# Six steps of 768 tokens instead of nine of 512 in the last phase of a fused attention and mixer kernel, with layer two after layer one and partly by seven block products

## The chip, the cores and the metric

The kernel runs on one core of a Trainium2 chip. The metric is the device time of one execution in microseconds (us); the median of three runs is shown beside a profile of one execution. The engines are TensorE (PE; PEld is its weight load, which runs beside the matmuls), VectorE (DVE), ScalarE (ACT), GpSimd (POOL) and SyncE (SP). In this kernel POOL and SP mostly issue transfers (DMAs).

## The reference

Three stages follow each other on 8 sequences of 576 tokens and 512 channels, all in float32:

```
p_packed = softmax(p k^T / 8) v          # 32 packed keys per head, 8 heads of 64
x        = softmax(q p_packed^T / 8) p_packed
xk, xr   = mu * x + (1 - mu) * x_prev    # x_prev: the token before
x        = sigmoid(xr @ w_r) * (relu(xk @ w_k)^2 @ w_v)         # 512 -> 1024 -> 512
u        = x + (x^T @ U @ V)^T           # mixing over tokens, rank 32
out      = u + relu(u @ w_ch1) @ w_ch2   # 512 -> 2048 -> 512
```

## The kernel before

The work stands in one program whose order is set by a planner (class `Plan`). The program adds operations with the tiles that they read and write; `emit` then plays a list schedule over its own estimates of durations and transfer times, and each engine gets its instructions in the order in which that schedule took them. An engine keeps to its order at run time, so an instruction that is not ready holds all that stand behind it. A tile pool with n buffers gives out its oldest buffer again when the readers of the old tile are done.

Every float32 operand of a large product is split into a high and a low part of type fp32r (`split`: a copy, mostly on ACT, and a subtraction on DVE), and each product runs three passes, high by high, high by low, low by high (`PASS`).

*Phase 1* (0 to about 697 us) is attention and the first mixer, in 12 chunks of 384 token columns. Its last chunks also prepare the last phase: the float64 weights are cast, and `make_ws` forms seven combinations of 128 x 256 blocks of `w_ch1` per pair f of hidden blocks, splits them and stores them in DRAM (`ws_d`).

*Phase 2* (from about 697 us) is the last two lines of the reference, over 36 tiles of 128 tokens in `NQ` = 9 steps q of four tiles. `load_u`, `h_block` and `t_block` (lines 1280 to 1329) bring x, add the token mixing (tile names psh, u) and turn u so that channels lie on partitions (ux, uq_d, ut; in the first step by matmuls, pst); `operands` (L1331) forms seven combinations of half-size blocks and splits them (ob). Then, for each f of 8 (loop at L1526):

- Layer one is a 2 x 2 block product with seven products in place of eight. `product` (L1355) does one as 6 matmuls (2 halves of the contraction by 3 passes) of 256 columns: 128 hidden units by 256 tokens, the weights (tile wb) from `ws_d`, 256 KB for each product, issued by POOL into a ring of 11 buffers (`load_ws`, L1246). Sums and copies of the seven results (tile tmp) give the four blocks of the hidden layer.
- `hidden` (L1370) applies relu and splits each block (tile hid).
- Layer two is plain: `c2_block` (L1378) multiplies a block of hid by the 128 x 512 rows of `w_ch2`, which are split once and stay in SBUF (w2). These are 3 passes of 512 columns per token tile and hidden block, accumulated over the 16 hidden blocks in four PSUM banks that hold a whole step.

So one f is 42 matmuls of 256 columns and 24 of 512, and both kinds stand side by side in PE's order: layer two of one f is done with layer one of the next. In the profile psc names the PSUM tiles of both layers.

## Time and profile before

| | |
|---|---|
| three runs | 1465.65, 1471.7 and 1472.11 us, median 1471.7 |
| profiled execution | span 1469.3 us from the first to the last instruction; no time around the span is given |
| PE busy | 1435.3 us, 98% of the span, 9104 matmuls |
| PEld, DVE, ACT busy | 85%, 67% and 49% of the span |
| psc matmuls | 1728 of 512 columns (layer two) and 3024 of 256 columns (layer one) |
| DMA | 294.53 MB; 132.15 MB of them by POOL's queue |

How to read it. The mean of one matmul is its length from start to end, and neighbours overlap; what one costs in a stream is the distance from start to start. Busy time of a group is the union of its matmuls' spans. A wait is named by what ended it. The share of DMA is summed over queues, so it can pass 1 when two queues have packets under way on the same engine.

### The profile page before, as it was taken

How to read it: one execution, taken by the hardware profiler on the slowest of the kernel's cores; microseconds unless marked ns; L12 is line 12 of the kernel's file. 1: busy time of each engine (PE TensorE's matmuls, PEld its weight loads, DVE VectorE, ACT ScalarE, POOL GpSimd, SP SyncE). 2: the span in 40 equal slices, each digit the busy share in tenths (PEclk: the TensorE clock that was granted, in tenths of full speed). 3: DMA queues.
4: the chain of work that ended last, by engine and by line, in shares of the span. 5: the costliest groups of instructions: out<-in, count | busy, mean ns of one | idle time of the engine just before them, and what ended most of it. 6: DMA issues, size and time to landing. Idle time of an engine off the chain costs nothing.

```text
span 1469.3 us, 25583 instructions
## 1 busy us (share of the span) xinstructions
PE 1435.3 (98%) x9104; PEld 1254.8 (85%) x9104; DVE 987.4 (67%) x2142; ACT 713.9 (49%) x1522; POOL 269.4 (18%) x519
## 2 busy tenths in 40 slices
PE   6789999999999999999999999999999999999998
PEld 5557988788888888888999999999999999999997
DVE  6877977788798888895665565556546554554633
ACT  5668656666676677764443333323333332323322
POOL 0000000000000000010333333333333343333331
PEclk9989999999999999999999999999999999999999
DMA  8963344655654477791999898899988889879763
GB/s 230 244 182 145 109 106 119 201 162 150 181 154 149 149 236 266 249 279 46 315 267 241 224 232 219 214 256 232 229 225 216 206 214 252 209 215 236 202 177 81
DMA packets 235725, 294.53 MB, mean 200 GB/s; under 512 B 91216, under 2 KB 126352, under 8 KB 235600
## 3 DMA queue, kind: packets, MB, share of 16 engines
q1 hardware_dynamic: 163024, 160.76, 37.9%
q0 software_dynamic: 72576, 132.15, 35.8%
q8 instruction: 73, 1.20, 0.4%
q14 instruction: 52, 0.43, 0.1%
HBM read 231.94 MB, written 60.89 MB: 199 GB/s over the span
## 4 chain that ended last, share of the span: by engine, by line
PE 90%; DVE 3%; DMA 3%; ACT 1%; SPq 1%; issue 1%; DVEq 0%; ACTq 0%
PE psc L197 51%; PE psv L197 12%; PE psk L197 12%; PE psr L197 6%; PE psat L197 4%; PE psat L209 2%; SPq L319 1%; DMA st<-in_moe_w_k_dram 1%; PE psu L197 1%; DMA w_d<-m 1%; PE psh L197 1%; DMA kin<-in_k_dram 0%; ACT a L233 0%; DMA st<-in_moe_w_ch_dram 0%; DVE a L264 0%
## 5 line engine op out<-in xcount | busy, mean ns | idle before, releaser
L197 PE MATMUL psc<-w,hid 128*128 128x512 f32 x1728 | 420.1, 391 | 0.0
L197 PEld LDWEIGHTS psc<-ob,wb 128*128 128x128 f32 x3024 | 387.1, 191 | 13.3
L197 PE MATMUL psc<-ob,wb 128*128 128x256 f32 x3024 | 391.6, 283 | 0.0
L319 POOL DMA_DIRECT2D wb<-ws_d x504 | 267.4, 531 | 647.0 <-PE psc L197 375.4
L197 PEld LDWEIGHTS psc<-w,hid 128*128 128x128 f32 x1728 | 314.8, 188 | 59.7 <-DVE hid L273 0.3
L233 ACT ACTIVATE hid<-tmp 128x256 fp32r<-128x256 f32 x216 | 131.3, 675 | 231.1 <-DVE tmp L254 231.1
L197 PE MATMUL psk<-xk,wk 128*128 128x384 f32 x1056 | 205.2, 339 | 0.1
L197 PE MATMUL psv<-wv,kk 128*128 128x512 f32 x783 | 201.5, 394 | 0.0
L197 PEld LDWEIGHTS psk<-xk,wk 128*128 128x128 f32 x1056 | 185.4, 188 | 9.7 <-issue 1.9
L197 PEld LDWEIGHTS psv<-wv,kk 128*128 128x128 f32 x783 | 144.4, 188 | 28.9 <-issue 0.8
L273 DVE SCALAR_TENSOR_TENSOR hid<-tmp,hid 128x256 fp32r<-128x256 f32 x216 | 126.7, 633 | 54.8 <-ACT hid L233 54.1
L273 DVE SCALAR_TENSOR_TENSOR hid<-psc,hid 128x256 fp32r<-128x256 f32 x72 | 45.3, 629 | 170.3 <-ACT hid L233 170.3
L254 DVE TENSOR_TENSOR tmp<-tmp,psc 128x256 f32<-128x256 f32 x288 | 112.9, 409 | 60.2 <-PE psc L197 59.8
L233 ACT ACTIVATE hid<-psc 128x256 fp32r<-128x256 f32 x72 | 45.8, 636 | 158.5 <-PE psc L197 158.5
L197 PE MATMUL psr<-wr,xr 128*128 128x512 f32 x414 | 110.7, 403 | 0.2
L197 PEld LDWEIGHTS psr<-wr,xr 128*128 128x128 f32 x414 | 76.5, 191 | 18.5 <-issue 1.7
L288 ACT ACTIVATE tmp<-psc 128x256 f32<-128x256 f32 x144 | 57.2, 397 | 59.4 <-PE psc L197 51.5
L233 ACT ACTIVATE sq<-psk 128x384 f32<-128x384 f32 x96 | 46.4, 489 | 68.1 <-PE psk L197 67.5
L311 POOL MEMSET x<- 128x8 f32 x4 | 0.5, 113 | 384.8 <-DVE m L270 384.5
L254 DVE TENSOR_TENSOR kk<-sq,kk 128x384 fp32r<-128x384 f32 x87 | 47.5, 550 | 26.7 <-ACT kk L288 26.4
L270 DVE SCALAR_TENSOR_TENSOR m<-x,mu_t,m 128x384 f32<-128x384 f32 x88 | 52.0, 607 | 2.3 <-ACT m L233 2.2
L233 ACT ACTIVATE m<-x,om_t 128x384 f32<-128x384 f32 x88 | 50.6, 606 | 4.0 <-DVE xr L254 2.9
(176 smaller groups left out, 1590.4 us busy)
## 6 DMA issues: line engine op xcount, KB each, us to landing
wb<-ws_d POOLq DMA_DIRECT2D x504, 256.0 KB, 4.0
st<-in_moe_w_ch_dram SPq DMA_DIRECT2D x32, 512.0 KB, 5.1
ws_d<-wb SPq DMA_DIRECT2D x56, 256.0 KB, 3.6
x_d<-xo SPq DMA_DIRECT2D x16, 576.0 KB, 3.7
x_d<-x SPq DMA_DIRECT2D x36, 256.0 KB, 2.6
kin<-in_k_dram SPq DMA_DIRECT2D x32, 256.0 KB, 4.9
vin<-in_v_dram SPq DMA_DIRECT2D x32, 256.0 KB, 5.5
w_d<-m SPq DMA_DIRECT2D x32, 256.0 KB, 4.0
```

The source lines that it names most:

```text
L197: self.nc.tensor.matmul(o, l, r, start=start, stop=stop, **k)
L209: self.nc.tensor.transpose(out.get(), in_.get(), ident.get())
L233: self.nc.scalar.activation(o, in_.get(), func, **k)
L254: return self.elem(engs, lambda e, o, x, y: e.tensor_tensor(out=o, in0=x, in1=y, op=op), out, [a, b], self.TT, cls)
L270: ("dve",), lambda e, o, x, y, z: e.scalar_tensor_tensor(out=o, in0=x, scalar=z, in1=y, op0=op0, op1=op1), out, [a, b, s], {"dve": (1.042, ...
L273: ("dve",), lambda e, o, x, y: e.scalar_tensor_tensor(out=o, in0=x, scalar=s, in1=y, op0=op0, op1=op1), out, [a, b], self.TT, cls)
L288: self.nc.scalar.activation(o, i, AF.Copy)
L311: (self.nc.gpsimd if eng == "pool" else self.nc.vector).memset(o, 0.0)
L319: (self.nc.sync if eng == "sp" else self.nc.gpsimd).dma_start(out=o, in_=i)
```

## The change

Phase 2 goes in `NS` = 6 steps s of six tiles (768 tokens); a token half is three tiles, 384 columns.

- `window_a` does layer one of a whole step first: the same seven products per f, 6 matmuls of 384 columns each. The hidden blocks stay in SBUF as float32 (tile hid; blocks 11, 12, 21, 22 are token half by hidden block of the pair, for four groups g of two f). The moving operand is now read as three tiles of 32-element pieces (t, a, r).
- Layer two follows. In steps 0 and 1 `window_b_plain` does it as before, 512 columns a pass, with `w2` loaded and split again in each of these steps, and beside it `make_t` forms seven combinations per pair of `w_ch2` blocks and stores them in DRAM (`t_d`).
- In steps 2 to 5 `window_b` does it by seven block products in seven stages (PSUM tiles psX, psY, psZ, psW). A stage is four units g; a unit splits one 128 x 768 hidden combination (`halves_split`, tile sp, 3 buffers) and runs 18 matmuls of 256 columns. The weights come from `t_d`. Sums over hidden blocks (hid) run ahead of the stages, and `into` adds results to u in SBUF after a stage.
- Weights of both layers come in transfers of 512 KB (two products or one unit) into a ring of 6 buffers (`load_w`).
- The operands of the next step (`operand_steps`) are formed at the end of `window_a` and through layer two. Phase 1 keeps its matmuls; tiles of weights share pools in groups (wA, wB, wC), mixed inputs are allotted in pairs, and six u tiles in place of four are prepared before phase 2.

In PE's order, one f of phase 2 stood like this before (a stretch past the middle; hid and wb name the operands of layer two and layer one):

```order
L197 MATMUL psc_11704<-ob,wb 128x256 x6
L197 MATMUL psc_11713<-ob,wb 128x256 x6
L197 MATMUL psc_11753<-ob,wb 128x256 x6
L197 MATMUL psc_11131<-w_10_8099,hid 128x512 x3
L197 MATMUL psc_11145<-w_10_8099,hid 128x512 x3
```

At the passage from layer one to layer two of a late step it now stands like this (ring is a weight transfer, sp a split hidden combination):

```order
L197 MATMUL psc_13571<-ob,ring 128x384 x6
L197 MATMUL psX<-ring,sp 128x256 x5
L197 MATMUL psc_13570<-ob,ring 128x384 x6
L197 MATMUL psX<-ring,sp 128x256 x67
L197 MATMUL psY<-ring,sp 128x256 x58
L197 MATMUL psX<-ring,sp 128x256 x2
L197 MATMUL psY<-ring,sp 128x256 x14
L197 MATMUL psX<-ring,sp 128x256 x38
L197 MATMUL psZ<-ring,sp 128x256 x2
L197 MATMUL psX<-ring,sp 128x256 x18
L197 MATMUL psZ<-ring,sp 128x256 x2
L197 MATMUL psX<-ring,sp 128x256 x14
```

The two layers no longer alternate. Where two or so matmuls of a later stage stand in the middle of psX, the planner saw psX not ready there.

On DVE, one f of phase 2 stood like this before (tmp are sums of layer one, hid the low parts of the split, u and ux the preparation of the next step):

```order
L254 TENSOR_TENSOR tmp<-tmp,psc_14997 128x256
L273 SCALAR_TENSOR_TENSOR hid<-psc_14988,hid 128x128x2
L254 TENSOR_TENSOR tmp<-tmp,psc_14997 128x256
L254 TENSOR_TENSOR tmp<-tmp,psc_15030 128x256
L254 TENSOR_TENSOR tmp<-tmp 128x256
L273 SCALAR_TENSOR_TENSOR hid<-tmp,hid 128x128x2 x2
L254 TENSOR_TENSOR tmp<-tmp,psc_14997 128x256
L254 TENSOR_TENSOR u<-psh,u 128x512
```

In the second and third stage of a late step DVE now has this (sp is the low part of a split, hid a sum over hidden blocks, u a result added):

```order
L254 TENSOR_TENSOR sp<-hid,sp 128x768 x2
L254 TENSOR_TENSOR u<-u,psX 128x2x256 x2
L273 SCALAR_TENSOR_TENSOR hid<-hid 128x768
L254 TENSOR_TENSOR u<-u,psX 128x256 x2
L254 TENSOR_TENSOR sp<-hid,sp 128x768
L273 SCALAR_TENSOR_TENSOR hid<-hid 128x768
L254 TENSOR_TENSOR u<-u,psX 128x2x256
L254 TENSOR_TENSOR sp<-hid,sp 128x768
L254 TENSOR_TENSOR hid<-hid 128x768
L254 TENSOR_TENSOR u<-u,psX 128x256
L273 SCALAR_TENSOR_TENSOR sp<-hid,sp 128x768
L273 SCALAR_TENSOR_TENSOR hid<-hid 128x768
```

Between two splits that PE waits for stand sums that are needed later only. The core of the diff:

```diff
-    NQ = NBP * NI // 4
-    vx_p, st_p, wb_p, tr_p = rpools = [Pool(bufs=n) for n in (1, 6, 11, 3)]
+    NS = NBP * NI // 6
+    ring_p, vx_p, st_p, turn_p = rpools = [Pool(bufs=n) for n in (6, 1, 4, 1)]
...
+    def put_split(homes, src, dst):
+        if not piece:
+            piece.extend(pieces(*next(homes)))
+        t, hi, lo = piece.pop(0)
+        split(hi, lo, src)
+        plan.dma(dst, t.rearrange("p a c -> p (a c)").bitcast(F32))
+
...
+    def make_t(f, homes):
+        homes = iter(homes)
+        b11, b12, b21, b22 = [t[:, h * 256:(h + 1) * 256] for t in raw_pair(w2_d, f) for h in range(2)]
+        t1, t2, t3, t4 = [temp("sums")[:, 0:256] for _ in range(4)]
+        plan.tt(t1, b12, b11, sub)
+        plan.tt(t2, b22, t1, sub)
+        plan.tt(t3, b12, b22, sub)
+        plan.tt(t4, b21, t2, sub)
+        g, h = divmod(f, 2)
+        for i, src in enumerate((b11, b21, b22, t4, t1, t2, t3)):
+            put_split(homes, src, t_d[i][g].at(h)[:, h * 512:(h + 1) * 512])
-    def load_ws(f, i):
-        t = plan.tile(wb_p, [P, 2, 256], F32R, "wb", parts=(0, 1))
-        plan.dma(t.rearrange("p a c -> p (a c)"), ws_d[f].at(i)[:, i * 512:(i + 1) * 512], eng="pool")
-        return t
+    def load_w(src):
+        t = plan.tile(ring_p, [P, 2, 2, 256], F32R, "ring")
+        plan.dma(t.rearrange("p n a c -> p (n a c)"), src, eng="pool")
+        return t
...
-        ops[q] = [o11] + [whole(x) for x in (t2, t1, b21, b12, b22, b11)]
+        for i, src in enumerate((b11, t2, t1, b21, b12, b22, b11)):
+            yield
...
+            if i == 6:
+                plan.tt(b11, b21, t2, sub)
+            hi, lo = [half(t, n).rearrange("p (a c) -> p a c", a=4) for n in range(2)]
+            plan.cls = 2 if s and i > 2 else 1
+            plan.copy(hi, src, ("act",) if s else ("act", "dve"))
+            plan.tt(lo, src, hi, sub)
+            plan.cls = 1
+            ops[s].append(t)
...
-        n = 0
-        for k in range(2):
-            for wi, a in PASS:
-                plan.mm(ps, half(w, wi)[:, k * P:(k + 1) * P],
-                        half(x, a).rearrange("p (a k c) -> p k a c", a=4, k=2)[:, k],
+    def product(s, f, i, ps, fresh):
+        n, e = divmod(ws_at[f, i], 2)
+        if e == 0:
+            wpair[0] = load_w(ws_d[n])
+        w, x = wpair[0][:, e], ops[s][i]
+        out = ps[:, 0:CW]
+        c = 0
+        for k in range(2):
+            for wi, a in PASS:
+                plan.mm(out, w[:, wi, k * P:(k + 1) * P],
+                        half(x, a).rearrange("p (a k t r) -> p k t a r", a=4, k=2, t=3)[:, k],
+                        start=(fresh and c == 0), stop=(c == 5), skip_group_check=True)
+                c += 1
+        return out
...
-    def hidden(src):
-        t = plan.tile(mix_p, [P, 2, CW], F32R, "mx", parts=(0, 1), name="hid")
-        hi, lo = [half(t, i)[:, 0:256].rearrange("p (t c) -> p c t", t=2) for i in range(2)]
-        src = src.rearrange("p (c t) -> p c t", t=2)
-        plan.act(hi, src, AF.Relu)
-        plan.stt(lo, src, 0.0, hi, ALU.max, sub)
-        return t
+    def window_a(s, prep):
+        hb = {}
...
+        for f in range(NF):
+            g, e = divmod(f, 2)
+            h11, h12, h21, h22 = [hb[b, g][e] for b in ("11", "12", "21", "22")]
+            ba = new_bank("psc1")
+            a = product(s, f, 0, ba, True)
+            p1, p5 = temp("p1"), temp("p5")
+            plan.copy(p1, a, ("act",))
+            if last:
+                tail(*last)
+            bb = new_bank("psc1")
+            b = product(s, f, 1, bb, True)
+            plan.tt(h21, p1, b, add)
+            bc = new_bank("psc1")
+            c = product(s, f, 2, bc, True)
+            plan.copy(p5, c, ("act",))
+            product(s, f, 3, ba, False)
+            plan.act(h11, a, AF.Relu)
+            product(s, f, 4, bb, False)
+            plan.tt(h22, p1, b, add)
+            plan.tt(h22, h22, p5, add)
+            product(s, f, 5, bc, False)
+            plan.tt(h21, h21, c, add)
+            if s >= NPLAINB:
+                plan.stt(h21, h21, 0.0, h11, ALU.max, sub)
+            last = (f, bb, p1)
+            for fn in prep.get(f, ()):
+                fn()
+        tail(*last)
+
+    def halves_split(src, relu):
+        t = plan.tile(sp_p, [P, 2, 768], F32R, "sp", parts=(0, 1))
+        hi, lo = [half(t, n).rearrange("p (f c) -> p f c", f=2) for n in range(2)]
+        if relu:
+            plan.act(hi, src, AF.Relu)
+            plan.stt(lo, src, 0.0, hi, ALU.max, sub)
+        else:
+            plan.copy(hi, src, ("act",))
+            plan.tt(lo, src, hi, sub)
+        return [half(t, n) for n in range(2)]
...
-        for t in range(2):
-            for i, (a, wi) in enumerate(PASS):
-                plan.mm(acc[q, th][t], half(h, a)[:, t * P:(t + 1) * P], half(w, wi),
-                        start=(fresh and i == 0), stop=(last and i == 2))
+        def into(u, col, name, op=add):
+            cs = slice(col * 256, (col + 1) * 256)
+            x = accs[name]
+            u01, u2 = u[0][:, :, cs], u[1][:, cs]
+            plan.tt(u01, u01, x[0].rearrange("p (t c) -> p t c", t=2), op)
+            plan.tt(u2, u2, x[1][:, 0:256], op)
...
+        stages = (("X", 0, "11", True), ("Y", 6, "21", True), ("X", 1, "12", False), ("Z", 4, "11", True),
+                  ("Y", 3, "22", False), ("Z", 5, "21", False), ("W", 2, "12", True))
+        for n, (name, ti, blk, fresh) in enumerate(stages):
+            if fresh:
+                accs[name] = [new_bank("ps" + name) for _ in range(2)]
+            acc = accs[name]
+            for g in range(NF // 2):
+                h11, h12, h21, h22 = [hb[b, g][2] for b in ("11", "12", "21", "22")]
+                if n == 3:
+                    plan.tt(h11, h21, h11, add)
+                elif n == 6:
+                    plan.stt(h12, h12, 0.0, h21, ALU.max, sub)
+                x = halves_split(hb[blk, g][2], n in (2, 4))
+                if n == 2:
+                    plan.stt(h21, h22, 0.0, h21, ALU.max, add)
+                w = load_w(t_d[ti][g])
+                for e in range(2):
+                    for t in range(3):
+                        o = acc[t // 2][:, t % 2 * 256:(t % 2 + 1) * 256]
+                        for c, (a, wi) in enumerate(PASS):
+                            plan.mm(o, x[a][:, e * CW + t * P:e * CW + (t + 1) * P], w[:, e, wi],
+                                    start=(fresh and g == 0 and e == 0 and c == 0 and t != 1),
+                                    stop=(g == NF // 2 - 1 and e == 1 and c == 2), skip_group_check=True)
+            if n == 0:
+                into(u0, 1, "X")
+                into(u1, 0, "X")
+                into(u1, 1, "X")
+            elif n == 1:
+                into(u1, 1, "Y")
+            elif n == 2:
+                into(u0, 0, "X")
+            elif n == 3:
+                into(u1, 0, "Z", sub)
...
+            next_op()
...
+                    x = halves_split(hb[("11", "12", "21", "22")[2 * th + k], g][2], (th, k) != (0, 0))
+                    for e in range(2):
+                        for t in range(3):
+                            for c, (a, wi) in enumerate(PASS):
+                                plan.mm(acc[3 * th + t], x[a][:, e * CW + t * P:e * CW + (t + 1) * P], half(w[e], wi),
+                                        start=(g == 0 and k == 0 and e == 0 and c == 0),
+                                        stop=(g == NF // 2 - 1 and k == 1 and e == 1 and c == 2))
+                next(more, None)
+                if k == 0 and NPLAINB < NS:
+                    make_t(s * NF // NPLAINB + g, [(3, sp_p, "sp")] + [(2, ust_p, "ust")] * 2)
...
-    for q in range(NQ):
-        for f in range(NF):
+    for s in range(NS):
+        prep = {f: [] for f in range(NF)}
+        more = iter(())
+        if s + 1 < NS:
+            T0 = 6 * s + 6
+            for T in range(T0, T0 + 6):
+                load_u(T)
+            for n in range(6):
+                T = T0 + n
+                if T % NI == 0:
+                    prep[n].append(lambda T=T: load_xu(T // NI))
+                prep[n + 1].append(lambda T=T: h_block(T))
+                prep[n + 2].append(lambda T=T: t_block(T))
+        window_a(s, prep)
+        if s + 1 < NS:
+            more = operand_steps(s + 1)
+            next(more)
+        (window_b if s >= NPLAINB else window_b_plain)(s, more)
+        for _ in more:
+            pass
```

## Rows read from the trace of the kernel before

**Rows 1.** From the page: busy time of each engine, share of the span, instructions.

```profile
PE 1435.3 (98%) x9104; PEld 1254.8 (85%) x9104; DVE 987.4 (67%) x2142; ACT 713.9 (49%) x1522; POOL 269.4 (18%) x519
```

**Rows 2.** The chain that ended last: start us, us, what, number of matmuls.

```profile
177.76 4.18 PE psk L197 x24
...
725.07 10.52 PE psc L197 x66
...
746.58 52.59 PE psc L197 x330
```

**Rows 3.** PE's groups by form: matmuls, columns, count, busy us, mean ns, idle us.

```profile
L197 PE MATMUL psc<-w,hid 128*128 128x512 f32 x1728 | 420.1, 391 | 0.0
L197 PE MATMUL psc<-ob,wb 128*128 128x256 f32 x3024 | 391.6, 283 | 0.0
L197 PE MATMUL psk<-xk,wk 128*128 128x384 f32 x1056 | 205.2, 339 | 0.1
```

**Rows 4.** PE in time order, fourth step: start us, us, what, count.

```profile
1001.88 0.40 PE L197 MATMUL psh<-X,vst 128*128 128x512 f32 x1
1002.11 2.32 PE L197 MATMUL psc<-ob,wb 128*128 128x256 f32 x18
1004.27 2.91 PE L197 MATMUL psc<-w,hid 128*128 128x512 f32 x12
1007.02 2.31 PE L197 MATMUL psc<-ob,wb 128*128 128x256 f32 x18
1009.17 2.91 PE L197 MATMUL psc<-w,hid 128*128 128x512 f32 x12
```

**Rows 5.** POOL's waits: us in total, times, longest.

```profile
POOL wb L319 <- PE psc L197: 375.4, 145, 45.2
```

**Rows 6.** Stretches: busy us of each engine (instructions), clock, DMA share, GB/s.

```profile
697.00:734.00 37.00, 37.00 (x234) 33.41 (x233) 24.28 (x51) 16.26 (x33) 13.75 (x26) 1.00 1.13 310
734.00:770.00 36.00, 36.00 (x230) 32.77 (x229) 22.77 (x48) 14.54 (x30) 12.70 (x24) 1.00 1.13 264
868.00:953.00 85.00, 85.00 (x533) 77.00 (x532) 45.79 (x97) 27.86 (x54) 29.61 (x56) 1.00 0.87 222
```

**Rows 7.** DMA queues from 703 to 715 us: packets, bytes, mean rate.

```profile
DMA packets 2338, 4.22 MB, mean 352 GB/s; under 512 B 285, under 2 KB 285, under 8 KB 2337
```

**Rows 8.** DMA issues: count, size of each, median us to landing.

```profile
wb<-ws_d POOLq DMA_DIRECT2D x504, 256.0 KB, 4.0
...
uq_d<-ux SPq DMA_DIRECT2D x16, 512.0 KB, 5.1
...
xa<-xu_d SPq DMA_DIRECT2D x32, 64.0 KB, 5.8
```

**Rows 9.** DVE's groups by form: shape, count, busy us, mean ns, idle us.

```profile
L254 DVE TENSOR_TENSOR tmp<-tmp,psc 128x256 f32<-128x256 f32 x288 | 112.9, 409 | 60.2 <-PE psc L197 59.8
...
L254 DVE TENSOR_TENSOR kk<-sq,kk 128x384 fp32r<-128x384 f32 x87 | 47.5, 550 | 26.7 <-ACT kk L288 26.4
...
L254 DVE TENSOR_TENSOR u<-psh,u 128x512 f32<-128x512 f32 x36 | 24.6, 683 | 0.6 <-PE psh L197 0.4
L254 DVE TENSOR_TENSOR u<-psc,u 128x512 f32<-128x512 f32 x36 | 24.5, 688 | 17.7 <-PE psc L197 17.6
...
L215 DVE STREAM_TRANSPOSE ux<-u 128x512 f32<-128x512 f32 x32 | 22.3, 696 | 0.1
...
L254 DVE TENSOR_TENSOR ob<-sums,ob 128x512 fp32r<-128x512 f32 x18 | 12.3, 687 | 0.0
...
L254 DVE TENSOR_TENSOR a<-a,s 128x640 f32<-128x640 f32 x8 | 6.5, 816 | 0.1
```

**Rows 10.** DVE in time order, back to back: start us, us, what.

```profile
650.76 0.68 DVE L254 TENSOR_TENSOR x<-psv,r 128x512 f32<-128x512 f32 x1
651.36 0.68 DVE L254 TENSOR_TENSOR xa<-xa,xb 128x512 f32<-128x512 f32 x1
651.96 0.55 DVE L254 TENSOR_TENSOR xr<-m,xr 128x384 fp32r<-128x384 f32 x1
```

More of the change, by code (lines that the diff above doesn't have):

```diff
@@ L163, in tile, with bank @@
         return v
-    def bank(self, group, name, ordered=True):
+    def bank(self, group, name, ordered=True, after=()):
         v = VTile((0,))
@@ L946, in packed_attention_moe_mixer_kernel, with wgroup, half @@
     w1b = Pool()
-    def wtile(pl, name):
-        return plan.tile(pl, [P, 2, 512], F32R, name, parts=(0, 1))
+    def wgroup(pl, name, n):
+        t = plan.tile(pl, [P, n, 2, 512], F32R, name, parts=tuple(range(2 * n)))
+        return [tuple(t.at(2 * i + a)[:, i, a, :] for a in range(2)) for i in range(n)]
+    def half(t, i):
+        return t[i] if isinstance(t, tuple) else t.at(i)[:, i, :]
     cast_cls = [0]
@@ L963, in cast_rows @@
         plan.cls = cast_cls[0]
-        last = cv.run([(slice(0, P), src)], 512, parts=[t.at(i)[:, i, :] for i in range(2)])
+        last = cv.run([(slice(0, P), src)], 512, parts=[half(t, i) for i in range(2)])
         plan.cls = 0
         return last
-    wr = [wtile(w1a, f"wr{j}") for j in range(NJ)]
-    wk = [[wtile(w1a, f"wk{j}_0")] for j in range(NJ)]
+    wr = wgroup(w1a, "wA", 3)
+    wB = wgroup(w1a, "wB", 3)
+    wr.append(wB[0])
+    wk = [[t] for t in wB[1:] + wgroup(w1a, "wC", 2)]
     plan.cls = 0
@@ L1087, in mix @@
         if dst is None:
-            dst = plan.tile(mix_p, [P, 2, CW], F32R, "mx", parts=(0, 1), name=("xk", "xr")[which])
+            if not mix_pair:
+                t = plan.tile(mix_p, [P, 2, 2, CW], F32R, "mx", parts=(0, 1, 2, 3), name=("xk", "xr")[which])
+                mix_pair.extend(tuple(t.at(2 * e + a)[:, e, a, :] for a in range(2)) for e in range(2))
+            dst = mix_pair.pop(0)
         xm[n, which, j] = dst
-        split(dst.at(0)[:, 0, :], dst.at(1)[:, 1, :], f)
-    def half(t, i):
-        return t.at(i)[:, i, :]
+        split(half(dst, 0), half(dst, 1), f)
     def r_block(n, t):
@@ L1470, in packed_attention_moe_mixer_kernel @@
             if kind == "k":
-                if n + 1 == len(chunks) and prep0:
-                    prep0.pop(0)()
+                for _ in range(1 if n + 2 >= len(chunks) else 0):
+                    if prep0:
+                        prep0.pop(0)()
                 k_block(n, m)
@@ L1501, in packed_attention_moe_mixer_kernel @@
+        if n == len(chunks) - 3:
+            for T in range(6):
+                load_u(T)
+            prep0 = [lambda T=T: h_block(T) for T in range(6)]
+        if n == len(chunks) - 2:
+            while prep0:
+                prep0.pop(0)()
+            prep0 = [lambda T=T: t_block(T) for T in range(6)]
         if n == len(chunks) - 1:
-            operands(0)
-            for m in range(3):
-                load_w2(m)
+            while prep0:
+                prep0.pop(0)()
+            for _ in operand_steps(0):
+                pass
```

358 lines of the change are left out of this document (169 added, 189 removed).

## The prediction

> **What bounds the kernel now.** I read the page first: PE is busy for 98% of the span, and no other engine passes 85% [rows 1]. The chain of waits then shows what the PE time of phase 2 is made of: pieces of 10.52 us with 66 matmuls, one behind the other, and longer runs of the same pace (52.59 us for 330) [rows 2]. That is one f after another, without a gap. PE's groups have no idle time before either kind of psc matmul [rows 3]. So phase 2 lasts as long as its matmuls take, and a change there is worth the PE time that it takes out, less the new waits.
>
> What a matmul costs in a stream is read from starts, not from its mean. In the fourth step, 18 matmuls of 256 columns start at 1002.11 and the next kind at 1004.27, 12 of 512 columns then take until 1007.02, and the next 18 until 1009.17 [rows 4]. That gives 2.155 us / 18 = 119.7 ns for 256 columns and 2.75 us / 12 = 229.2 ns for 512. The check: 42 x 119.7 + 24 x 229.2 = 10.53 us, the 10.52 us of the chain [rows 2]. For 384 columns phase 1 has the row: 24 psk matmuls in 4.18 us, 174.2 ns [rows 2, 3]. All three are columns at 2.4 GHz plus 13 to 16 ns; the granted clock is full in these stretches [rows 6].
>
> The other resources have room. POOL's loads wait for PE to free a buffer, 375.4 us in all, so they are early and not late [rows 5]. DVE is busy for 45.79 us of a step of 85 us [rows 6].
>
> **The change, part by part.**
>
> *Layer one.* 3024 matmuls of 256 columns become 6 x 8 x 7 x 6 = 2016 of 384. The columns stay the same, 1008 matmuls' overheads go: 3024 x 119.7 = 362.0 us becomes 2016 x 174.2 = 351.2 us, so -10.8 us. One thing is not shown by a row: the moving operand is read in runs of 32 elements, before in runs of 64. The nearest rows from both sides are the 384 columns read in one run, 174.2 ns, and the 256 columns read in runs of 64, which cost 13 ns over their columns, no more than whole ones [rows 2, 4]. I take 174.2; above it I keep 10% (17 ns, so +35 us) as the far end, below it nothing, since the columns themselves take 160 ns.
>
> The Trainium skill, "TensorE: Matmul & The Clock Gate", section "Back-to-back issue gap", gives N / 2.4 + 2.5 ns as the warm distance of lone matmuls. By it layer one would give back only 3 us, because there is little overhead to save, and both layers together 31 us; the rows here show 13 to 16 ns over the columns, and the sum goes by them.
>
> *Layer two.* Steps 0 and 1 keep 288 matmuls of 512 columns each; steps 2 to 5 take 7 x 4 x 18 = 504 of 256 each. 1728 x 229.2 = 396.1 us becomes 576 x 229.2 + 2016 x 119.7 = 132.0 + 241.3 = 373.3 us, so -22.8 us. The 256-column matmul here has the form of layer one's before (a 128 x 128 weight load for each), so its price has a row.
>
> Together PE loses 33.6 us of work. The token mixing keeps its matmuls (psh, 0.23 us each [rows 4]); eight more transposes in the first step cost under 1 us.
>
> *DVE in layer two by seven products.* Here the change adds waits. A 768-element operation is not in the trace; 512 elements take 687 ns and 640 take 816 [rows 9], 1.01 ns an element, so 945 ns standing alone. Back to back the next one starts 0.60 us after a 0.68 us one [rows 10], so 0.87 us in a stream. One window of layer two has 28 splits, 12 sums over hidden blocks, 11 operations for the next operands, and 11 additions into u (688 and 409 ns [rows 9], 0.93 us a pair in a stream): 51 x 0.87 + 11 x 0.93 = 54.6 us against 504 x 119.7 = 60.3 us of PE. On average that fits; in the middle it does not. A stage of PE is 8.6 us. In DVE's order, what stands from the first psX addition, ready at about 8.8 us, to the last split of the third stage is 14 long operations and 4 pairs, 15.9 us, so that split is ready at 24.7 us; PE wants it at 3 x 8.6 - 2.15 = 23.7 us. Counted on in the same way, the first two splits of the fourth stage come 1.5 to 2 us late. Only 3 split tiles exist, so DVE can't work further ahead. Bounds: nothing, if DVE keeps its pace and PE fills in with the few matmuls that the order shows there; 5 us a window, if each operation takes its 945 ns. I take 2 us, 8 us for four windows.
>
> *Plain steps.* Beside 66 us of PE, DVE has 16 splits, 16 low parts of w2 (687 ns), 44 operations of make_t on 256 elements (409 ns), 11 for operands and 6 additions: 27 x 0.87 + 22 x 0.6 + 44 x 0.33 = 51 us. It fits with room; 0 to 2 us a step, and I take 0.
>
> *Layer one on DVE.* Per f five additions and one subtraction on 384 elements (550 ns [rows 9]), 3.3 us of 7.3 us; with u and the turns (683 and 696 ns) 35 us of 60. Nothing waits.
>
> *The passage from phase 1.* The first operands need 11 DVE operations, 9.6 us, after the last transposes; in PE's order 42 psv matmuls, 42 x 0.229 = 9.6 us, stand behind these. So between 0 and 9.6 us; with the first operand needing only half of the tiles I take 2 us.
>
> *DMA.* A ring buffer is refilled while five others are used, 2.1 us each, so 10.5 us for a landing that takes 5.1 us for 512 KB [rows 8]. The rate is the question. A step by seven products moves 56 x 0.524 MB of weights, 6.3 MB of u in four passes and 0.7 MB of xu (16 pieces of 64 KB for nine tiles [rows 8]): 36.4 MB in 58.5 + 60.3 + 1.5 = 120.3 us, 302 GB/s, and in its first half up to 345. Before, a step ran at 222 GB/s [rows 6]. The trace has 352 GB/s over 12 us and 310 over 37 us without a wait of PE [rows 6, 7]. The ring (3.1 MB) carries the first half's excess over 310, 35 GB/s x 60 us = 2.1 MB. I take 0 us; the other end is a rival below. In POOL's order single w2 loads stand between ring loads of the first step; one that waits holds the ring, for less than the 10.5 us ahead.
>
> *Sum.* -33.6 + 8 + 2 = -23.6 us on the profiled execution, whose span is 1469.3 us: 1445.7. The median of the runs stands 2.4 us above that span, so 1448 us.
>
> **The rivals.**
>
> - *No new wait.* DVE's lateness is swallowed and the passage is covered: 1471.7 - 33.6 = 1438 us. For it: before, DVE's splits never held PE in phase 2 [rows 3]. Against: DVE's room falls from 46% to 10% in these windows.
> - *DVE becomes the bound.* Every operation costs its lone 945 ns, 5 us late in each of four windows, 3 in each plain step, and the passage costs 5: -33.6 + 31 gives 1469 us, no change. For it: the order's interleaved psX rows. Against: the pace of rows 10.
> - *DMA becomes the bound, and the kernel is slower.* The place is the four steps by seven products. At a rate r each takes 36.4 MB / r; the gain is gone when that passes 120.3 + 33.6 / 4 = 128.7 us, so below 283 GB/s. In the stretch from 734 to 770 us the DMA share was 1.13 and 264 GB/s were moved [rows 6]. At that rate each of these steps takes 137.9 us and a plain one (35.3 MB) 133.7 instead of 126: 4 x 17.6 + 2 x 8 - 33.6 = +53 us, 1525 us. Against: PE did not wait there, so 264 may be all that was asked, and rows 7 show more.
> - *The 384-column matmul is dearer with 32-element runs.* +17 ns on 2016 takes the gain: 1448 + 35 = 1483 us, slower. Against: runs of 64 cost nothing [rows 4].
>
> **How the numbers follow.** Forecast 1448 us, 0.50 (its own range 1438 to 1458); no wait 0.21; DVE 0.13; DMA 0.10; dear matmul 0.06. A measurement of this kernel can tell about 0.5%, 7.4 us. Faster by more than that (under 1464.3): 0.50 + 0.21 + a third of the DVE case and a part of a mild DMA case, 0.78. Within: most of the DVE case and a little of the others, 0.11. Slower: 0.11. The range is 1433 to 1469: its lower end is 5 us under the no-wait case for what the pairing of tiles in phase 1 may bring, its upper end takes in the DVE case; DMA and the dear matmul, in their full size, are left out.
>
> **What would show it.** Right: psc matmuls of 384 columns 174 ns apart; psX to psW 120 ns apart; a window of layer two 62 to 63 us, with PE waiting for DVE sp at the third and fourth stage; POOL's ring loads still waiting for PE. Wrong: PE waiting for DMA ring (the DMA case); starts 190 ns apart in layer one (the dear matmul); PE waits in the plain steps or in phase 1, for which I counted nothing; a window under 61 us, which would mean that DVE was never late.

## The result and the profile after

The changed kernel takes 1477.2 us (median of 6 runs, 1475.8 to 1482.8), the kernel before 1471.3 us beside it: a ratio of 1.0053, 95% interval 1.0038 to 1.0068. The forecast was 1448 us. So some 24 us of gain did not come, and 6 us were lost.

The profiled execution is the slowest of the six and has a span of 1481.0 us. Phase 1 ends at 697 us as before; the difference lies behind it. The engines' row answers to [rows 1], PE's groups to [rows 3], VectorE's to [rows 9]:

```profile
PE 1425.4 (96%) x8968; PEld 1288.6 (87%) x8968; DVE 1084.6 (73%) x2107; ACT 708.9 (48%) x1421; POOL 167.9 (11%) x327
...
L197 PE MATMUL psc<-ob,ring 128*128 128x384 f32 x2016 | 375.1, 345 | 17.9 <-DVE hid L254 14.7
...
L254 DVE TENSOR_TENSOR sp<-hid,sp 128x768 fp32r<-128x768 f32 x88 | 83.3, 952 | 28.7 <-ACT sp L288 28.7
```

PE's share falls from 98% to 96%, and layer one's matmuls, which had no idle time before them, have 17.9 us. Where it lies shows in a table by window: a window of layer one, then one of layer two, for the six steps (length, busy us of PE, PEld, DVE, ACT, POOL with instructions, clock, DMA share, GB/s), as [rows 6]:

```profile
697.00:764.00 67.00, 64.46 (x354) 62.71 (x353) 45.09 (x78) 24.84 (x47) 14.55 (x28) 1.00 0.95 271
764.00:828.00 64.00, 64.00 (x284) 53.08 (x283) 44.73 (x89) 23.43 (x40) 10.08 (x19) 1.00 0.72 231
828.00:897.00 69.00, 63.93 (x342) 62.97 (x342) 36.40 (x64) 19.03 (x38) 13.27 (x25) 0.95 1.05 286
897.00:962.00 65.00, 65.00 (x290) 53.99 (x289) 47.82 (x97) 23.99 (x40) 8.06 (x15) 1.00 0.74 219
962.00:1038.00 76.00, 67.48 (x352) 65.50 (x351) 44.20 (x77) 18.89 (x34) 14.84 (x28) 0.93 1.10 301
1038.00:1099.00 61.00, 60.50 (x498) 60.01 (x497) 48.47 (x67) 22.03 (x27) 14.83 (x28) 1.00 0.84 241
1099.00:1163.00 64.00, 62.39 (x346) 60.74 (x345) 37.58 (x65) 17.04 (x31) 14.83 (x28) 1.00 1.19 318
1163.00:1227.00 64.00, 61.80 (x504) 60.83 (x503) 52.02 (x70) 24.82 (x30) 14.84 (x28) 1.00 0.85 242
1227.00:1291.00 64.00, 62.35 (x347) 60.80 (x347) 36.69 (x65) 15.89 (x29) 14.84 (x28) 1.00 1.16 317
1291.00:1353.00 62.00, 61.52 (x508) 61.12 (x507) 51.46 (x70) 24.83 (x30) 14.83 (x28) 1.00 0.89 253
1353.00:1413.00 60.00, 60.00 (x339) 60.00 (x338) 28.26 (x52) 14.31 (x27) 14.83 (x28) 1.00 0.90 267
1413.00:1474.00 61.00, 60.54 (x505) 60.32 (x503) 43.68 (x60) 21.15 (x25) 12.18 (x23) 1.00 0.78 220
```

Layer two came as forecast: 64 and 65 us for the plain steps, 61, 64, 62 and 61 us for those by seven products (forecast 66, and 62 to 63). Layer one did not. The last window, in which no next step is prepared, takes 60 us where 336 x 174.2 ns = 58.5 us were reckoned; those of steps 1 and 2 take 69 and 76 us. In these two PE is idle for 5.1 and 8.5 us, and its mean granted clock is 0.95 and 0.93, which by length times missing clock is 3.5 and 5.3 us more (an estimate from these rows). What PE waits for in phase 2 (total, times, longest us):

```profile
PE psc L197 <- DVE hid L254: 14.7, 5, 5.1
PE psc L197 <- DMA ring<-ws_d: 1.8, 4, 0.8
PE psZ L197 <- ACT sp L288: 1.8, 4, 0.5
...
PE psX L197 <- DVE sp L273: 1.1, 1, 1.1
PE psX L197 <- DVE sp L254: 0.7, 1, 0.7
```

The ring costs 1.8 us, layer two's splits (sp) 1.8 us behind ACT and 1.8 us behind VectorE; these matter little. It is the sums of hidden blocks, in layer one, where the forecast had VectorE half idle. PE in time order, at its two long waits, at the end of a layer two by seven products (as [rows 4]), and in the last layer one:

```profile
853.56 6.26 PE L197 MATMUL psc<-ob,ring 128*128 128x384 f32 x21 [5.07 <-DVE hid L254]
...
985.34 2.30 PE L197 MATMUL psc<-ob,ring 128*128 128x384 f32 x12
992.68 7.32 PE L197 MATMUL psc<-ob,ring 128*128 128x384 f32 x24 [5.04 <-DVE hid L254]
...
1090.50 8.80 PE L197 MATMUL psW<-ring,sp 128*128 128x256 f32 x72
1099.14 2.13 PE L197 MATMUL psc<-ob,ring 128*128 128x384 f32 x11
...
1352.92 60.08 PE L197 MATMUL psc<-ob,ring 128*128 128x384 f32 x336
1412.84 2.44 PE L197 MATMUL psX<-ring,sp 128*128 128x256 f32 x19
```

From start to start, 72 psW take 8.64 us, 120 ns each, as forecast. But 336 psc take 59.92 us, 178.3 ns each and not 174.2. And behind a 5 us wait 24 matmuls take 7.3 us, where 4.3 us would do: the granted clock is down. (A bracket at the end of a row is the idle time before it and what ended it.) VectorE just before the wait that ends at 992.68:

```profile
985.48 0.69 DVE L254 TENSOR_TENSOR xa<-xa,xb 128x512 f32<-128x512 f32 x1 [3.02 <-DMA xb<-xu_d]
...
986.67 0.56 DVE L273 SCALAR_TENSOR_TENSOR hid<-hid 128x384 f32<-128x384 f32 x1
990.42 0.69 DVE L254 TENSOR_TENSOR u<-psh,u 128x512 f32<-128x512 f32 x1 [3.19 <-DMA u<-x_d]
991.02 0.54 DVE L254 TENSOR_TENSOR hid<-p,psc 128x384 f32<-128x384 f32 x1
991.49 0.70 DVE L215 STREAM_TRANSPOSE turned<-u 128x512 f32<-128x512 f32 x1
992.11 0.51 DVE L254 TENSOR_TENSOR hid<-p,psc 128x384 f32<-128x384 f32 x1
```

VectorE stands for 3.0 and 3.2 us before operations whose loads have not landed (xb, a part of xu, and u), and the sum that PE waits for is queued behind the second. The Trainium skill ("PSUM — Partial Sum Buffer", section "Engine vs sequencer instructions") says that VectorE's queue is strictly first in, first out. The trace agrees: PE had been done at 987.6, and the sum that released it ran at 992.1, behind the addition into u, another sum and a turn of u. So an engine busy for 44 of 76 us held the bound one. Why is u late? SyncE's queue around the start of that window (start us, us, what, count):

```profile
947.51 3.67 SPq L319 DMA_DIRECT2D t_d<-bl  x5
951.27 0.57 SPq L319 DMA_DIRECT2D xa<-xu_d  x1
...
964.18 4.66 SPq L319 DMA_DIRECT2D out_dram<-u  x5
968.93 0.43 SPq L319 DMA_DIRECT2D xa<-xu_d  x1
...
970.83 6.31 SPq L319 DMA_DIRECT2D out_dram<-u  x6
977.20 0.57 SPq L319 DMA_DIRECT2D xb<-xu_d  x1
...
981.69 3.52 SPq L319 DMA_DIRECT2D u<-x_d  x5
```

Layer one begins at 962 us, the first u load is issued at 981.7. Ahead of it stand 11 stores of the step before, whose buffers these loads take, at 1 us each, the loads of xu, and two pairs of stores of t_d. A load then takes its time to land (issues in phase 2: size, median us; [rows 8] have 5.1 us for a larger one):

```profile
u<-x_d SPq DMA_DIRECT2D x46, 128.0 KB, 9.8
```

This queue is that of step 2. In step 1, whose wait is as long, the queue is shorter: the first load of u is issued 6 us into layer one (833.9 us), in step 3, which has no such wait, 4 us into it (1103.5). But VectorE comes to its first addition into u 16 us into layer one in step 1 (843.5) and 19 us in step 3. Between load and addition lie 9.6 and 14.9 us, against landings of 10.3 and 11.2 us (medians of the two windows). So it is the place in VectorE's order as much as the queue.

The planner that writes the order reckons with 0.3 us for an issue and about 3 us for a landing (`LOADED`), so it puts the additions into u where they would be ready by these numbers.

### The profile page after: what moved, and what is told of

The parts are those of the page before. It is cut to its first block, busy times and chain, and to the rows that moved or that the text cites. A ratio compares the mean times of both kernels' runs of the same rounds, so it can differ in the third digit from the quotient of the medians.

```text
span 1481.0 us, 24613 instructions
## 1 busy us (share of the span) xinstructions
PE 1425.4 (96%) x8968; PEld 1288.6 (87%) x8968; DVE 1084.6 (73%) x2107; ACT 708.9 (48%) x1421; POOL 167.9 (11%) x327
## 4 chain that ended last, share of the span: by engine, by line
PE 72%; DMA 9%; issue 9%; DVE 6%; POOL 2%; ACT 1%; SPq 1%; POOLq 0%; DVEq 0%; ACTq 0%
PE psc L197 18%; PE psk L197 13%; PE psv L197 12%; PE psr L197 7%; PE psZ L197 5%; PE psat L197 4%; PE psY L197 4%; PE psX L197 3%; PE psat L209 3%; POOL ring L319 2%; PE psW L197 2%; DMA u<-x_d 1%; SPq L319 1%; PE psu L197 1%; DMA ring<-ws_d 1%
## 5 line engine op out<-in xcount | busy, mean ns | idle before, releaser
L197 PE MATMUL psc<-ob,ring 128*128 128x384 f32 x2016 | 375.1, 345 | 17.9 <-DVE hid L254 14.7
L197 PEld LDWEIGHTS psc<-ob,ring 128*128 128x128 f32 x2016 | 365.0, 191 | 24.6 <-DVE hid L254 17.4
L197 PE MATMUL psv<-w,kk 128*128 128x512 f32 x783 | 200.1, 395 | 0.0
L197 PEld LDWEIGHTS psv<-w,kk 128*128 128x128 f32 x783 | 144.4, 188 | 29.2 <-issue 1.2
L319 POOL DMA_DIRECT2D ring<-ws_d x168 | 89.4, 532 | 471.9 <-PE psc L197 259.5
L197 PE MATMUL psc<-w,sp 128*128 128x512 f32 x576 | 131.6, 389 | 0.0
L197 PEld LDWEIGHTS psc<-w,sp 128*128 128x128 f32 x576 | 108.1, 188 | 22.0
L288 ACT ACTIVATE sp<-hid 128x768 fp32r<-128x768 f32 x88 | 74.3, 844 | 89.1 <-PE psX L197 38.2
L197 PE MATMUL psk<-xk,w 128*128 128x384 f32 x528 | 103.9, 339 | 0.1
L197 PEld LDWEIGHTS psk<-xk,w 128*128 128x128 f32 x528 | 92.8, 188 | 5.0 <-ACT w L288 0.6
L233 ACT ACTIVATE sp<-hid 128x768 fp32r<-128x768 f32 x56 | 47.2, 845 | 92.7 <-PE psc L197 34.0
L197 PEld LDWEIGHTS psr<-wA,xr 128*128 128x128 f32 x315 | 58.5, 191 | 15.4 <-DVE xr L291 1.5
```

What stands on the lines that cost most here:

```text
L197: self.nc.tensor.matmul(o, l, r, start=start, stop=stop, **k)
L233: self.nc.scalar.activation(o, in_.get(), func, **k)
L288: self.nc.scalar.activation(o, i, AF.Copy)
L319: (self.nc.sync if eng == "sp" else self.nc.gpsimd).dma_start(out=o, in_=i)
```

## The experiments

**Theory.** The loads of u for the next step come late; VectorE, in order, meets the additions that need them before their data and holds the sums that PE waits for; the clock then falls. Apart from that the 384-column matmul is dearer. **Rival:** the DMA's rate in layer one (286 to 318 GB/s) makes everything late in whatever order. Ratios are to the kernel before on the same chip; the change has 1.0053. Window lengths here run from the first to the last matmul of layer one (74 and 77 us for steps 1 and 2 of the change, since the planner lets the last ones stand among those of layer two) and are from the profiles, one execution of each kernel. These differ by some us, and a profiled execution can lie far from its median: that of e9 is the fastest of its ten (1461.8 us), those of e3 and e7 are the slowest of theirs (1482.9 and 1482.7 us). Part of that is phase 1, which no edit concerns: its first 115 us have a mean granted clock of 0.82 in e3's profile, 0.88 in the change's and 0.96 in e11's.

**e1: operands in one run.** The hi and lo parts are written in the order in which the matmul reads them.

```diff
-hi, lo = [half(t, n).rearrange("p (a c) -> p a c", a=4) for n in range(2)]
+hi, lo = [half(t, n).rearrange("p (q a r) -> p a q r", q=6, a=4) for n in range(2)]
+src = src.rearrange("p a (q r) -> p a q r", q=6)
...
-half(x, a).rearrange("p (a k t r) -> p k t a r", a=4, k=2, t=3)[:, k],
+half(x, a)[:, k * CW:(k + 1) * CW],
```

> The operands of layer one are laid out so that each 384-column matmul reads its columns in one run, not in runs of 32. If the 32-element runs are what makes it dearer (178.3 ns between starts, against 174.2 ns of the psk matmul with the same columns), starts come 174 ns apart and 2016 x 4.1 ns = 8 us go: 1469 us, ratio to before 0.998. If something else makes it dearer (the ring's landing beside it, the two operands), starts stay at 178 ns and the time at 1477 us. Either way the two 5 us waits at the start of the layer-one windows of steps 1 and 2 stay.

1474.0 us, 1.0023 (1.0003 to 1.0043). PE in the last layer one:

```profile
1349.92 58.41 PE L197 MATMUL psc<-ob,ring 128*128 128x384 f32 x336
1408.17 4.11 PE L197 MATMUL psX<-ring,sp 128*128 128x256 f32 x33
```

58.25 / 336 = 173.4 ns: the runs of 32 elements were the cause, 4.9 ns a matmul, 1.7 us a window, 10 us in all. Only some 4 us show in the time; the long waits of steps 1 and 2 stay (windows of 74 and 76 us).

**e2: later landings for the planner.**

```diff
+LATE = (300.0, 100.0, 1.19, 9000.0)
...
-issue, gap, share, land = self.LEAD if t < self.CHUNKS else self.LOADED
+issue, gap, share, land = self.LEAD if t < self.CHUNKS else (
+    self.LOADED if t < 715000.0 else self.LATE)
```

> Order alone: the planner is told that a transfer of phase 2 lands 9 us after its turn on the wire, not 3 us, so VectorE's additions of the token mixing (u<-psh,u) are put further back in its order. Theory (late loads of u hold VectorE, which runs in order, and behind it the sums that TensorE waits for): the two 5 us waits and the clock dips behind them go, 15 to 20 us in all, 1457 to 1463 us. Rival (the layer-one windows are bound by the rate of the DMA, whatever the order): at most 5 us go, 1472 us or more, and the waits turn up at the ring.

1490.8 us, 1.0142 (1.0109 to 1.0175): a miss on both sides. The price holds for the ring's weights and for xu too, so the whole order changed; PE now waits 8.3 us for one addition into u and 11.6 us for ACT's copies of p1, and the two windows take 75 and 79 us. It speaks for neither theory; it shows only that the order alone moves 14 us.

**e3: all six steps plain; e6: the same with e1.** `NPLAINB` is 6 and not 2.

> All six steps do layer two by plain products; layer one as in the change. By the seven-product steps' measured windows (61.4 us against 66 plain) the four steps give up 4 x 4.6 = 18 us: 1495 us if nothing else moves, which the rival (DMA rate in the seven-product steps) would lower to about 1490 with the layer-one windows of steps 3 and 4 under 64 us. The theory of late loads of u says more: a plain step stores all six tiles at its very end, and the two windows with 5 us waits are those behind plain steps; with six plain steps the windows of steps 3 and 4 and 5 get that wait too, 5 to 8 us each for steps 3 and 4: 1505 to 1511 us.

1471.2 us, 1.0010 (0.9994 to 1.0026): a miss, slower by neither number, but faster than the change by 6 us, though four of its layer-two windows have some 4 us more of PE's work each. The part of the theory that blamed the stores at the end of a plain step falls: the windows of steps 1 and 2, behind plain steps here too, take 62 and 63 us and have no long wait. PE waits for `hid` 5.3 us in all of phase 2, the longest wait (3.5 us) in step 3. SyncE's queue at the same step:

```profile
958.09 7.75 SPq L319 DMA_DIRECT2D out_dram<-u  x11
965.89 13.06 SPq L319 DMA_DIRECT2D u<-x_d  x12
```

The stores stand there as before, but neither stores of t_d nor loads of xu between them, and u is issued at 966, 16 us earlier.

> All six steps plain (1471 us in e3_plain), with the operands in one run. The 4 ns per 384-column matmul, 8 us, come off, since little else waits there: 1463 us. If the gain of the operands' layout is swallowed by waits, 1468 us or more.

1467.2 us, 0.9971 (0.9953 to 0.9989): 0.4% under e3, 6 us of the 8 to 10.

**e4: no stores of the results of steps 0 to 3.** `send` returns at once for tiles under 24.

> Leaves out the stores of the results of steps 0 to 3 (the rows of those tokens in the output stay empty); everything else is kept. Theory: the loads of u for the next step wait for these stores to free their buffers; without them they land 7 to 10 us earlier, the 5 us waits in the layer-one windows of steps 1 and 2 go, 12 to 18 us: 1459 to 1465 us. Rival (rate): 4.7 MB less of 331 MB, 1% of the traffic, moves TensorE by 0 to 3 us: 1474 us or more.

1472.4 us, 1.0019 (1.0000 to 1.0037), 5 us less than the change, between the two. (The stores left out are 6.3 MB, 24 tiles of 262 KB, and not 4.7.) Step 1's window loses its wait (74 to 63 us), step 2's keeps it (74 us). The planner orders the rest anew here, so this is not a clean proof, but the stores have a part in step 1's lateness, and in step 2 something else holds u.

**e5: the token mixing one f later in the program.**

```diff
-prep[n + 1].append(lambda T=T: h_block(T))
-prep[n + 2].append(lambda T=T: t_block(T))
+prep[n + 2].append(lambda T=T: h_block(T))
+prep[min(n + 3, NF - 1)].append(lambda T=T: t_block(T))
```

> With the operands in one run, as in e1_runs (1474 us), and the token mixing of the next step moved back by one f: in the program's order each u block comes one f (7.3 us) later, its transposition too. Theory (the loads of u are issued late, behind stores and other transfers in SyncE's queue, and VectorE waits for them in order): the wait at the start of step 1's layer one (5 to 6 us) goes, that of step 2 shrinks by up to 7 us; 10 to 15 us less with the clock dips: 1459 to 1464 us. Rival (it is the DMA's rate, whatever VectorE waits for): 1471 us or more. A cost to look for: the transposed u reaches layer two's operand sums later, up to 5 us in each of five steps.

1479.9 us, 1.0064 (1.0042 to 1.0086): worse than e1. PE's wait between 828 and 1000 us is

```profile
PE psc L197 <- DVE hid L254: 16.6, 4, 7.7
```

The planner puts first on VectorE what it holds to be ready, not what comes first in the program; the additions hardly moved (in step 1 the first three run 16 to 21 us into the window, as in the change), and VectorE waits at three of them in a row for u in either window. Not a test of the theory.

**e7: xu of step 3 loaded a step earlier; e8: no stores of t_d in step 1.** Both with e1's layout.

```diff
-if T % NI == 0:
+if T % NI == 0 and n:
     prep[n].append(lambda T=T: load_xu(T // NI))
...
+if s + 1 < NS and (6 * s + 12) % NI == 0 and 6 * s + 12 < 6 * NS:
+    prep[7].append(lambda T=6 * s + 12: load_xu(T // NI))
 window_a(s, prep)
```

> As e1_runs (1474 us), with the 16 loads of xu for step 3's tokens put at the end of step 1's layer one instead of at the start of step 2's. Theory: in step 2's layer one these loads, which wait for buffers that the rewriting of w_ch2 still holds, stand in SyncE's queue before the output stores and the loads of u (issued 981 to 995 us, 20 us into the window); without them u is issued some 10 us earlier, and step 2's window falls from 75 us to 63 to 66 us: 1462 to 1466 us. Rival (the rate): the window stays over 71 us, 1470 us or more. Step 1's wait stays in either case.

> Leaves out the storing of w_ch2's blocks in step 1 (28 stores, 7.3 MB; layer two of steps 2 to 5 uses the blocks of step 0 in their place); the splits that make them are kept. If it is these stores in SyncE's queue and on the DMA that make step 2's loads late, its window falls from 75 us to 66 us or less, 1464 us; if it is the loads of xu, which stay, it stays over 70 us, 1469 us or more.

e7: 1473.8 us, 1.0027 (1.0000 to 1.0054); e8: 1469.6 us, 0.9977 (0.9957 to 0.9997), 0.46% under e1. By their stated bounds e7 speaks against the loads of xu as the cause (1470 us or more), e8 against the stores of t_d (1469 us or more). Step 2's window falls from 76 to 72 us in e7 and to 71 us in e8, in one execution each: neither is the cause alone, and what each is worth by itself is not shown. In e7 step 1's window grows from 74 to 77 us, and in step 2's PE's longest wait is 8.0 us, behind three additions into u; in e8 VectorE waits 4.4 us for xu in step 2's.

**e9: the additions held back; e10: and the xu loads moved.** The bank of a token mixing is granted only after `mark`, the last sum of f = HOLD[n], with HOLD = (3, 3, 4, 4, 5, 5). The loads of xu move back with it; no transfer is added or left out.

```diff
-prep[n + 1].append(lambda T=T: h_block(T))
-prep[n + 2].append(lambda T=T: t_block(T))
+f = HOLD[n]
+prep[f].append(lambda T=T: h_block(T, mark))
+prep[f].append(lambda T=T: t_block(T))
```

In e10, loads of xu are issued at f = 0 of their window, those for step 3 at f = 6 of step 1.

> As e1_runs (1474 us), but the planner may give the token mixing of the next step its bank only after the sums of f = 3, 3, 4, 4, 5, 5 (tiles 0 to 5), some 30 to 45 us into the layer-one window, so that on VectorE the additions into u stand behind more of the sums that TensorE waits for. Nothing about transfers changes. Theory (late u loads hold VectorE, and through it TensorE, because of their place in its order): the waits of 5 to 8 us in steps 1 and 2 go; step 1's layer one falls from 73 to 61 us, step 2's from 76 to 64 to 68 us (the loads of xu stay): 1450 to 1458 us. Rival (DMA rate): the windows stay over 70 us, 1470 us or more. Cost to look for: the operands of the next step come later, waits of psX or of the next layer one.

> As e9_hold, and the loads of xu for step 3's tokens stand in step 1's layer one (at f = 6), not in front of the stores and u loads of step 2; the others are issued at the start of their window. Theory: step 2's layer one falls to 61 to 63 us too, 1447 to 1453 us. If the xu loads cost nothing once VectorE doesn't wait early, no difference from e9_hold.

e9: 1472.2 us, 1.0025 (1.0000 to 1.0050); e10: 1464.1 us, 0.9964 (0.9939 to 0.9989). In the profiles step 1's window falls from 74 to 62 us (e9), as the theory says; its loads are issued much as before (the first of u 5 us into it, 6 us in e1). Step 2's falls only to 70 us in e9, and to 60 us in e10. What holds step 2 in e9 is not u but xu:

```profile
967.44 0.69 DVE L254 TENSOR_TENSOR xa<-xa,xb 128x512 f32<-128x512 f32 x1 [9.50 <-DMA xb<-xu_d]
```

PE waits 7.9 us behind it. So any load that is late for its first user on VectorE does it, not that of u alone. In e10 the loads of xu are out of the way, and the first load of u is issued 5 us into step 2's window, 18 us in e1: there the order of SyncE's queue was mended together with VectorE's. The times follow only in part; e9's median is where the rival had it. PE's waits in phase 2 of e10:

```profile
PE psX L197 <- DVE sp L273: 6.7, 6, 1.6
PE psY L197 <- DVE sp L254: 3.4, 1, 3.4
PE psZ L197 <- DVE sp L254: 2.9, 3, 1.5
```

The waits for `hid` are gone, waits in layer two have come. VectorE in e10, in layer two of step 3:

```profile
1160.46 0.96 DVE L254 TENSOR_TENSOR sums<-y 128x768 f32<-128x768 f32 x1 [3.91 <-DMA y<-uq_d]
```

The transposed u comes back later, and VectorE's work for the next operands now stands between the splits of the first four stages, where it has no time to spare, and waits there for y.

**e11: the operands' work gives way; e14: with the mixing of every second tile one f earlier.** All VectorE work on the next operands gets class 2, which the planner takes when nothing of class 1 is ready; it moves to the last three stages.

```diff
+plan.cls = 2 if s else 1
 plan.tt(t1, b12, b11, sub)
...
-plan.cls = 2 if s and i > 2 else 1
+plan.cls = 2 if s else 1
```

> As e10_hold_xu (1464 us), and all VectorE work on the next step's operands gives way to everything else that is ready; in the program's order it moves from the first four stages of a layer-two window to the last three. Theory: in e10 these operations stand in front of splits and sums that layer two's first stages wait for (15 us of waits of psX, psY and psZ in four windows, and a clock dip); they go mostly, 1450 to 1456 us. Rival: VectorE is short over the whole window, so the waits move to later stages or to the next layer one, 1461 us or more.

> As e11_hx_cls, with the token mixing one f earlier (sums of f = 2, 3, 3, 4, 4, 5). The transposed u comes back up to 7 us earlier, so the operand sums don't wait for it. If the u loads are in time by then: as e11 or up to 4 us less. If VectorE meets late u loads again: waits of 2 to 5 us in steps 1 and 2, 4 to 10 us more than e11.

e11: 1441.0 us (1438.6 to 1443.9), 0.9820 (0.9787 to 0.9853); e14: 1440.5 us, 0.9806 (0.9776 to 0.9836), no different. Both beat both kernels, and e11 gives more than expected. PE's longest waits in e11 are

```profile
PE psZ L197 <- ACT sp L288: 1.8, 4, 0.5
PE psc L197 <- DVE sp L254: 1.0, 1, 1.0
```

and its layer-one windows of steps 1 to 3, with the columns of the table above:

```profile
818.00:880.00 62.00, 61.50 (x349) 60.44 (x349) 35.19 (x65) 18.33 (x34) 14.12 (x27) 1.00 1.07 315
...
944.00:1005.00 61.00, 60.49 (x344) 59.10 (x343) 36.13 (x66) 14.36 (x27) 15.04 (x29) 1.00 1.12 311
...
1066.00:1127.00 61.00, 60.78 (x346) 59.55 (x345) 36.70 (x66) 14.99 (x28) 14.84 (x28) 1.00 1.09 308
```

The DMA moves 308 to 315 GB/s here, about what it did in the change's windows of 64 to 76 us (286 to 318), and PE is busy throughout at full clock. The rival falls. Nor do the loads of u land sooner (10.5 us, median of 46 in e11's phase 2, 9.8 in the change): what is gone is the user that stood too early in VectorE's order.

**e12: e10 with all steps plain.**

> As e10_hold_xu, with layer two plain in all six steps. The forecast's price of layer two (228 ns x 288 against 120 ns x 504 a step) says 22.8 us more PE work, and less of VectorE's lateness: 1464 + 23 - 15 = 1472 us by e10's own waits. If the seven-product layer two costs as much in waits and in its preparation as it saves, 1460 to 1466 us.

1456.0 us, 0.9914 (0.9886 to 0.9942), below every number expected: the waits of e10 lay in the seven-product windows, and with them gone PE waits 1.8 us in all. Against e11, where little waits either, layer two by seven products is worth 15 us. The forecast had 22.8 less 8 of lateness; the lateness is not there and the gain is smaller, so its net of 15 us agrees by luck.

**e13 and e15: e10 and e11 with runs of 32. e16: the change with e11's priority alone.**

> As e10_hold_xu, with the moving operand of layer one in runs of 32 elements, as in the change. If each of the 2016 matmuls costs 4.1 ns more (178.3 against 174.2 ns), 8 us more now that little waits there: 1472 us. If the extra hides in waits, 1464 to 1467 us.

> As e11_hx_cls (1441 us), with the moving operand of layer one in runs of 32 elements, as in the change. A window without preparation took 59.9 us with them against 58.2 us without (after against e1): 6 x 1.7 = 10 us, 1451 us, if nothing hides it; 1444 us if it shows as little as between e10 and e13 (3 us).

> The change itself (1477 us), with the operands' work of the next step giving way on VectorE; nothing else. Theory (the long waits come from late u loads that stand early in VectorE's order): the waits at the start of steps 1 and 2 stay, and layer two gets back the little it lost: 1470 to 1476 us. Rival (the operands' work is what makes VectorE late everywhere): 1460 us or less.

e13: 1467.5 us, 0.9990 (0.9971 to 1.0009), 3 to 4 us over e10. e15: 1450.8 us, 0.9869 (0.9842 to 0.9897), 10 us over e11, as expected. So the dear matmul costs its full price once nothing waits, and a third of it while VectorE sets the pace. e16: 1473.2 us, 1.0020 (1.0000 to 1.0039), as the theory said: 0.33% under the change; PE waits 17.2 us for `hid`. The priority does little without the later mixing (e16), the later mixing with the xu loads moved less than half without the priority (e13: 10 of the 27 us that e15 gains); together they give it all.

## Why the forecast was wrong, point by point

- *Layer one on DVE, "Nothing waits"*: this step failed. The sum of busy time was right (36 to 45 us of a window), but it does not tell whether an in-order engine is free when wanted. The forecast priced the operations, not where they stand in VectorE's order relative to their loads, those of u and of xu. Taken out by order alone, VectorE's and SyncE's (e13, e15, e16), it is worth 22 us from e16 to e15. In the change's profile it is 14 us of PE's idle time in steps 1 and 2 and 9 us of lowered clock, 22 us as well, of which the forecast had none.
- *DMA, "0 us"*: the rate was no bound, as reckoned, up to 318 GB/s; and the ring was far enough ahead (1.8 us of waits in layer one, 1.2 in layer two). What it left out is SyncE's queue: with six tiles a step, 11 stores and 12 loads stand behind one another, 21 us by e3's rows, where a step of the kernel before (868 to 953 or 953 to 1038 us) had 7 or 8 of each. The forecast counted bytes and the ring's buffers, not u's.
- *Layer one, 174.2 ns*: mis-sized. The row it used reads one run; with runs of 32 it is 178.3 ns, 8 us, and 10 us between e11 and e15. The forecast had this as a far end of +17 ns, and took the near end, +0, where 4 were measured.
- *Layer two, 119.7 ns*: right, 120 ns. But 512 columns alone cost 227 ns, not 229.2 (12 of them from 959.64 to 962.36 us in the change): the plain windows took 64 to 65 us, not 66, so the gain is 4 to 5 us a step, not 5.7; e12 against e11 gives 15 us, not 22.8.
- *DVE's lateness, 8 us in four windows*: PE waits 1.8 us for VectorE's splits there in the change, all of it in one window, and not at all in e11; in e10 it is 13 us. It depends on where the operands' work stands, not on the pace of a lone operation (952 ns, as reckoned, 0.87 in a stream).
- *The passage from phase 1, 2 us*: right only by luck. The first window has 2.5 us of idle time, by its row, but the first matmuls of layer one follow phase 1 without a wait; the idle time comes 19 to 30 us later, behind a copy, a load of the ring and a sum. *Plain steps, 0*: right.
- *The rivals*: "DVE becomes the bound" named the engine, but for its pace in layer two; VectorE was busy 73% and waiting. "DMA becomes the bound" and its break-even rate: shown wrong by e11. "The dear matmul": right in kind, 8 of its 35 us.
- *The sum*: 1448 + 8 (matmul) + 22 (waits and clock in steps 1 and 2) - 1 = 1477 us, the measured time; the 1 is what is left, not measured by itself. The 10 us of waits that 1448 holds are about met in total: by the table PE is idle for 23.0 us in phase 2, 9.4 of them outside these two windows, though mostly not at the places forecast. With the order mended and the operands as in the change (e15) the time is 1450.8 us, near the forecast, in part by luck: the dearer matmul, which was not counted, stands there for waits that were.

What stays open: why step 1's and step 2's waits are 5 us and not more or less, run by run. Of e10's loss to e11, 21 us in phase 2, 16 are idle time of PE (20.4 against 4.6 us from the first matmul of layer one to the last of layer two); 3.4 are two stretches of about 3.4 us at 0.50 of the clock in e10, around 704 and at 1164 us, counted half; the rest is not explained.

## What to carry to other kernels

An engine that is half idle can still be the one that holds the bound engine, if it works in order and something in its queue waits for a transfer: read, for every load of a stage, when it is issued (its queue, and whose buffer it takes), when it lands, and what stands behind its first user. When steps were made larger here, the transfers at a step's edge piled up on one queue, 11 stores and 12 loads where there had been 7 or 8 of each. And a wait that was moved off one stage (e10) turned up in the next one with no time to spare, so a mended order is judged by the sum of all windows, not by the window that was mended.

## What was not expected of the hardware

A pause of 5 us costs TensorE more than the pause: TensorE then runs for some us at 1.2 and not 2.4 GHz. The 10 us around the second pause have a mean granted clock of 0.66 (stretch, length, busy us, clock, DMA share, GB/s), four of them 0.50 with PE busy throughout, the whole window 0.93. Shorter waits can do it too: behind two of 2.5 and 0.7 us the clock from 971 to 975 us is 0.57.

```profile
990.00:1000.00 10.00, 7.32 (x25) 6.96 (x26) 6.43 (x12) 0.49 (x1) 0.53 (x1) 0.66 1.11 245
994.00:998.00 4.00, 4.00 (x15) 4.00 (x14) 1.82 (x4) 0.00 (x0) 0.53 (x1) 0.50 1.07 260
```

A moving operand read in 12 runs of 32 elements costs 4.9 ns a matmul of 384 columns over one run (178.3 against 173.4 ns), where the rows had shown no cost for runs of 64 [rows 4]. And a load of u, 128 KB, takes 9.8 us to land in the change's phase 2 (median; 264 GB/s on average, 286 and 301 in the two long windows), where it took 5.5 us in the kernel before's stretch from 955 to 1000 us, at 248 GB/s:

```profile
u<-x_d SPq DMA_DIRECT2D x8, 128.0 KB, 5.5
```

Why it takes longer is not shown.
